# Range check of the decays spread over the later blocks of the second feed-forward, and a prefetch hint on the branch over the general path

## The chip, the cores and the metric

The kernel runs on one core of one Trainium2 chip. The metric is device microseconds for one execution, lower is better. The core has a matrix engine (TensorE, PE in the rows; its weight loads are PEld), a vector engine (VectorE, DVE), a scalar engine (ScalarE, ACT), a general engine (GpSimd, POOL) and a queue engine (SyncE, SP) that issues most transfers. Each engine runs its own instructions in the order in which they stand.

## The reference

A recurrent attention over 768 steps feeds two feed-forward layers. What the change touches is the second feed-forward, and a check on the decays `w` of the recurrence:

```python
def _moe2_ref(x, w_in, w_out):          # x: 3072 x 320, d_ff 2048
    h = np.maximum(x @ w_in, 0.0)
    return (h * h @ w_out).astype(np.float32)
```

The decays are drawn as `rand * 0.1 + 0.85`. The kernel's fast path for the recurrence is meant for decays between 0.25 and 2.0. Outside of that, a slow general path must compute everything again, so the kernel has to look at every one of the 983,040 decays.

## The kernel before, in words

The recurrence, the first feed-forward and the decoding of the weights fill the first 720 us. The weights arrive as 64-bit numbers in tiles `raw`; ACT (L324, L325), DVE (L327, L329) and POOL (L331) turn each into a 32-bit tile `wst`, and ACT and POOL split this into a high and a low part (`wih`, `wil`, `wir` for the first matrix, `wuh`, `wul` for the second).

The second feed-forward runs over 6 token blocks `j` of 512 tokens, and in each over 16 slices `ff` of 128 hidden units. I call one (`j`, `ff`) a step. A step has two halves on PE. `b_h` computes the hidden slice in 8 matmuls into the tile `ph` (L366). ACT and DVE then make its square in two parts: ACT `r_` (L972), DVE `q_` (L973), ACT `rh` (L974), DVE `rl` (L975). `b_o` multiplies `rh` and `rl` with the second matrix in 12 matmuls into four output tiles `po` (L988). `b_o` of a step is written three steps behind its `b_h` (`LAG`). When the last slice of a block is in, the four `po` tiles are copied out to `ob` by DVE and ACT (L998). The last weight tiles are still being decoded while block 0 runs.

`b_load` fetches the tokens of the next block and `b_split` splits them into `xh`, `xl`, `xq` (ACT L353 and L355, DVE L354 and L356).

The check on the decays: `look(i)` loads one eighth of them into `w_` (two buffers) and finds least and largest with two reductions on DVE (L1017). `within()` folds these to one number for each partition (L1023 to L1025), sends it to memory as `ok_d` (L1028), reads it back as one `row` (L1029), and reduces the row to the flag `one` (L1031, L1032). The flag is loaded into a register of each engine (L1043), and `tc.If(fast == 0)` (L1056) branches over the general path.

The program's order within each engine is set by a scheduler, which takes priorities from the order of the code and moves an instruction ahead where its inputs allow. So `look` and `b_split`, written at later places, stand in DVE's order well before the steps beside which they are written.

Of the kernel before, what the change touches and what calls it, by code (L numbers as in the profile page):

```python
# [11 lines left out]
ALU = mybir.AluOpType  # L12
# [13 lines left out]
LEAST, MOST = 0.25, 2.0  # L26
# [33 lines left out]
GAPM = (1300, 900, 1700, 1300, 1600, 1000, 0, 2600)  # L60
GAPE = (1300, 2400, 1700, 1600, 1600, 1300, 1000, 2400)
CUT = (7, 18)
LOOK = (2, 0, 3, 2, 5, 2)
WB = (6, 8, 3)
BP = 6000
BB = (5, 4)
# [176 lines left out]
def body(tc, img, rv, rd, vn, vp, raw, w1, w2, w3t, wo, win, wo2, ident, maskt, out, dbg=None):  # L243
    nc = tc.nc
    mm = nc.tensor.matmul
    act, dve, pool, sp = nc.scalar, nc.vector, nc.gpsimd, nc.sync

    with (
# [12 lines left out]
        with right, tc.manual_schedule(engines={mybir.EngineType.PE}):  # L261
# [90 lines left out]
            def split_x(f2, r2, xh, xl, xq):  # L352
                act.copy(out=xh, in_=f2)  # L353
                dve.tensor_tensor(out=xl, in0=f2, in1=xh, op=ALU.subtract)  # L354
                act.copy(out=xq[:, 0], in_=r2)  # L355
                dve.tensor_tensor(out=xq[:, 1], in0=r2, in1=xq[:, 0], op=ALU.subtract)  # L356

            def dense(ps, w_, ff, xh, xl, xq, i0=0, i1=8):
                h, l, r = w_
                f = slice(128 * ff, 128 * ff + 128)  # L360
                seq = []
                for k in range(2):
                    seq += [(h[:, k, f], xh[:, k]), (h[:, k, f], xl[:, k]), (l[:, k, f], xh[:, k])]
                seq[5:5] = [(r[:, f], xq[:, 0]), (r[:, f], xq[:, 1])]
                for i in range(i0, i1):
                    mm(out=ps, lhsT=seq[i][0], rhs=seq[i][1], start=(i == 0), stop=(i == 7))  # L366
# [123 lines left out]
            with (  # L490
# [30 lines left out]
                q_ = {"prep": sp}  # L521
# [350 lines left out]
                for c in range(NCH):  # L872
                    last = c == NCH - 1
# [52 lines left out]
            def b_split(pl, j, bufs=2):  # L926
                xf, xr = xt[j]
                xh = pl.tile([128, 2, 512], F32R, name="xh2", bufs=bufs)
                xl = pl.tile([128, 2, 512], F32R, name="xl2", bufs=bufs)
                xq = pl.tile([128, 2, 512], F32R, name="xq2", bufs=bufs)  # L930
                split_x(xf, xr, xh, xl, xq)
                xt[j] = (xh, xl, xq)
# [23 lines left out]
        with (  # L956
            left,
            tc.tile_pool(name="mb", bufs=1, side="right") as mb,
            tc.tile_pool(name="ps_h", bufs=4, space=PSUM) as ps_h,
            tc.tile_pool(name="ps_o", bufs=1, space=PSUM) as ps_o,  # L960
        ):
            NB = NTOK // 512
            rr = {}

            def b_h(j, ff):
                ps = ps_h.tile([128, 512], F32, name="ph")
                dense(ps, (wih, wil, wir), ff, *xt[j])
                r_ = mb.tile([128, 512], F32, name="r_", bufs=2)
                q_ = mb.tile([128, 512], F32, name="q_", bufs=2)
                rh = mb.tile([128, 512], F32R, name="rh", bufs=4)  # L970
                rl = mb.tile([128, 512], F32R, name="rl", bufs=4)
                act.activation(out=r_, in_=ps, func=AF.Relu)  # L972
                dve.tensor_tensor(out=q_, in0=r_, in1=r_, op=ALU.mult)  # L973
                act.copy(out=rh, in_=q_)  # L974
                dve.tensor_tensor(out=rl, in0=q_, in1=rh, op=ALU.subtract)  # L975
                rr[ff] = (rh, rl)

            po = {}

            def b_o(j, ff, gs=range(4)):  # L980
                if ff == 0:
                    po[j] = [ps_o.tile([128, DM], F32, name=f"po{g}") for g in range(4)]
                rh, rl = rr[ff]
                for g in gs:
                    t = slice(128 * g, 128 * g + 128)
                    for i, (a_, b_) in enumerate(((rh[:, t], wuh[:, ff]), (rh[:, t], wul[:, ff]),
                                                  (rl[:, t], wuh[:, ff]))):
                        mm(out=po[j][g], lhsT=a_, rhs=b_, start=(ff == 0 and i == 0), stop=(ff == 15 and i == 2))  # L988
                if ff == 15:
                    for g in gs:  # L990
                        c = 4 * j + g
                        if j < NB - 1:
                            ob = mb.tile([128, DM], F32, name="ob", bufs=4)
                        else:
                            if g == 0:
                                po["ob"] = mb.tile([128, 4, DM], F32, name="oball", bufs=1)
                            ob = po["ob"][:, g]
                        (act.copy if g % 2 else dve.tensor_copy)(out=ob, in_=po[j][g])  # L998
                        if j < NB - 1:
                            sp.dma_start(out=out.rearrange("(b s) o -> b s o", b=B)[:, C * c:C * c + C], in_=ob)  # L1000
                    if j == NB - 1 and gs[-1] == 3:
                        for b in range(B):
                            (act if b % 2 else sp).dma_start(
                                out=out.rearrange("(b c s) o -> b s c o", b=B, s=C)[b][:, 4 * j:4 * j + 4],
                                in_=po["ob"][C * b:C * b + C])

            NW = 8
            nw = NU * S * D // 128 // NW
            low, high = (mb.tile([128, NW], F32, name=n, bufs=1) for n in ("low", "high"))

            def look(i):

                w_ = mb.tile([128, nw], F32, name="w_", bufs=2)
                sp.dma_start(out=w_, in_=raw[3].rearrange("u s d -> (u s d)").rearrange("(p f) -> p f", p=128)[
                    :, nw * i:nw * i + nw])
                for o, op in ((low, ALU.min), (high, ALU.max)):
                    dve.tensor_reduce(out=o[:, i:i + 1], in_=w_, axis=mybir.AxisListType.X, op=op)  # L1017

            def within():


                for o, op in ((low, ALU.min), (high, ALU.max)):
                    dve.tensor_reduce(out=o[:, 0:1], in_=o, axis=mybir.AxisListType.X, op=op)  # L1023
                dve.tensor_scalar(out=high[:, 0:1], in0=high[:, 0:1], scalar1=MOST, scalar2=None, op0=ALU.is_le)
                dve.scalar_tensor_tensor(out=low[:, 0:1], in0=low[:, 0:1], scalar=LEAST, in1=high[:, 0:1],  # L1025
                                         op0=ALU.is_ge, op1=ALU.mult)
                row = mb.tile([1, 128], F32, name="row", bufs=1)
                sp.dma_start(out=ok_d, in_=low[:, 0:1])  # L1028
                sp.dma_start(out=row, in_=ok_d.rearrange("p o -> o p"))  # L1029
                one = mb.tile([1, 1], mybir.dt.int32, name="one", bufs=1)  # L1030
                dve.tensor_reduce(out=row[:, 0:1], in_=row, axis=mybir.AxisListType.X, op=ALU.min)  # L1031
                dve.tensor_copy(out=one, in_=row[:, 0:1])  # L1032
                return one

            lag = []
            for j in range(NB):
                for ff in range(16):
                    if j == LOOK[0] and LOOK[1] <= ff < NW + LOOK[1]:
                        look(ff - LOOK[1])
                    if (j, ff) == LOOK[2:4]:  # L1040
                        fast = within()
                    if (j, ff) == LOOK[4:6]:
                        fast = nc.values_load(fast, min_val=0, max_val=1)  # L1043
                    if ff == 4 and j + 1 < NB:
                        b_load(mb, j + 1)
                    if ff == 12 and j + 1 < NB:
                        b_split(mb, j + 1)
                    b_h(j, ff)
                    lag.append((j, ff))
                    if len(lag) > LAG:  # L1050
                        b_o(*lag.pop(0))
            for g in range(4):
                with tc.high_priority(offset=FIRST * (4 - g)):
                    for it in lag:
                        b_o(*it, gs=(g,))
        with tc.If(fast == 0):  # L1056
            general(tc, raw, w1, w2, w3t, wo, win, wo2, ident, out)
        if dbg is not None:
            sp.dma_start(out=dbg["X"], in_=X_d)
# [57 lines left out]
```

## Time and profile before

| what | value |
|---|---|
| median of 3 runs | 1101.18 us (1099.33 to 1102.74) |
| profiled execution, its own time | 1096.26 us |
| its span, first to last instruction | 1094.4 us |
| PE busy | 922.8 us (84%) |
| DVE busy | 735.0 us (67%) |
| ACT busy | 454.1 us (41%) |
| POOL busy | 264.6 us (24%) |

All rows come from the one profiled execution. A busy share says how long an engine had work under way, not whether that work set the end. "idle before <-" in a row is the time that the engine stood still before it, and what ended the wait.

### The profile page before, as it was taken

What the parts mean: (1) busy time and instruction counts of PE and PEld (TensorE: products, weight loads), DVE (VectorE), ACT (ScalarE), POOL (GpSimd) and SP (SyncE); (2) the same over time, 40 slices, a digit from 0 to 9 for tenths busy, and PEclk for the clock granted to TensorE, in tenths of its full rate; (3) what the DMA queues carried; (4) which work ended last, traced back from release to release, by engine and by line L of the source; (5) the groups of instructions that cost most, each with busy time, mean ns of one, the idle gap of its engine ahead of it and who ended that gap; (6) DMA issues with size and microseconds to landing.
All of it is one profiled execution on the core that took longest, in us unless ns stands there. A gap on an engine that the chain in (4) does not pass through costs nothing.

```text
span 1094.4 us, 29719 instructions
## 1 busy us (share of the span) xinstructions
PE 922.8 (84%) x12240; PEld 826.5 (76%) x12240; DVE 735.0 (67%) x1467; ACT 454.1 (41%) x1022; POOL 264.6 (24%) x310
## 2 busy tenths in 40 slices
PE   1326766789979889987999989888989999999996
PEld 1224544588879878887898879777878989898985
DVE  7785989967975996788489434999834434343432
ACT  3423655443434433433343434766423334343331
POOL 0384777613121122312100000886200000000000
PEclk9999988889989989989999989999989999999999
DMA  8967767377656656756555442569300200000001
GB/s 225 272 193 220 206 200 194 93 203 195 150 146 162 173 142 184 190 136 161 140 132 116 118 107 58 152 170 203 90 25 5 50 1 25 1 25 1 23 2 27
DMA packets 214743, 134.48 MB, mean 123 GB/s; under 512 B 143415, under 2 KB 187576, under 8 KB 214184
## 3 DMA queue, kind: packets, MB, share of 16 engines
q1 hardware_dynamic: 214312, 132.18, 46.5%
q8 instruction: 98, 1.61, 0.6%
q10 hardware_dynamic: 288, 0.33, 0.1%
q14 instruction: 45, 0.37, 0.1%
HBM read 99.27 MB, written 33.19 MB: 121 GB/s over the span
## 4 chain that ended last, share of the span: by engine, by line
PE 36%; DVE 9%; DMA 3%; issue 3%; ACT 1%; POOL 1%; SPq 0%; DVEq 0%; ACTq 0%; POOLq 0%
PE po L988 14%; PE ph L366 13%; PE ab L366 4%; PE px L424 2%; PE pat L795 1%; DVE wst L329 1%; DVE wst L327 1%; PE pat L767 1%; DVE high L1017 1%; DVE rl L975 1%; DMA X_d<-yst 1%; DVE tmp L651 1%; DMA ok_d<-low 1%; DVE gl L404 1%; DVE T L654 1%
## 5 line engine op out<-in xcount | busy, mean ns | idle before, releaser
L988 PE MATMUL po<-wuh,rh 128*128 128x320 f32 x384 | 119.0, 312 | 4.7 <-DVE ob L998 3.3
L988 PE MATMUL po<-wuh,rl 128*128 128x320 f32 x384 | 114.3, 311 | 6.1 <-DVE rl L975 6.1
L988 PE MATMUL po<-wul,rh 128*128 128x320 f32 x384 | 118.9, 311 | 0.0
L403 ACT CAST gh<-g 128x256 fp32r<-128x256 f32 x96 | 38.9, 406 | 108.0 <-DVE g L398 107.7
L331 POOL TENSOR_TENSOR wst<-wst,raw 128x256 f32<-128x256 f32 (+1 forms) x72 | 70.2, 982 | 55.0 <-DVE wst L329 32.0
L988 PEld LDWEIGHTS po<-wuh,rh 128*128 128x128 f32 x384 | 72.9, 190 | 9.1 <-issue 3.8
L366 PE MATMUL ab<-xh,w1h 128*128 128x256 f32 x192 | 60.9, 317 | 22.2 <-DVE g L398 22.2
L988 PEld LDWEIGHTS po<-wuh,rl 128*128 128x128 f32 x384 | 71.8, 190 | 7.9 <-DVE rl L975 7.3
L366 PE MATMUL ph<-xh,wih 128*128 128x512 f32 x192 | 76.0, 396 | 1.6 <-POOL wst L331 1.6
L988 PEld LDWEIGHTS po<-wul,rh 128*128 128x128 f32 x384 | 73.0, 190 | 4.0
L366 PE MATMUL ph<-xh,wil 128*128 128x512 f32 x192 | 76.0, 396 | 0.0
L366 PE MATMUL ph<-xl,wih 128*128 128x512 f32 x192 | 75.7, 394 | 0.0
L651 DVE TENSOR_TENSOR tmp<-PT,T 128x31 f32<-128x31 f32 (+20 forms) x170 | 69.1, 407 | 3.4
L795 PE MATMUL pat<-YI,YR 128*40 128x72 f32 (+1 forms) x1536 | 56.8, 236 | 15.4 <-DVE qt L597 10.4
L654 DVE TENSOR_TENSOR T<-T,tmp 128x31 f32<-128x31 f32 (+20 forms) x170 | 67.5, 397 | 2.7
L795 PEld LDWEIGHTS pat<-YI,YR 128*40 128x40 f32 x1536 | 52.4, 124 | 20.3 <-DVE qt L597 11.7
L404 DVE TENSOR_TENSOR gl<-g,gh 128x256 fp32r<-128x256 f32 x96 | 46.4, 484 | 27.7 <-ACT gh L403 27.3
L424 PE MATMUL px<-wph,gh 128*128 128x320 f32 x192 | 64.8, 338 | 0.0
L424 PE MATMUL px<-wph,gl 128*128 128x320 f32 x192 | 61.0, 318 | 1.3 <-DVE gl L404 1.3
L397 ACT COPY a_sb<-ab 128x256 f32<-128x256 f32 x96 | 35.6, 371 | 63.0 <-PE ab L366 62.4
L424 PE MATMUL px<-wpl,gh 128*128 128x320 f32 x192 | 60.7, 316 | 0.0
L366 PE MATMUL ph<-xq,wir 128*128 128x512 f32 x192 | 60.3, 394 | 0.0
(535 smaller groups left out, 2519.3 us busy)
## 6 DMA issues: line engine op xcount, KB each, us to landing
im<-img SPq DMA_DIRECT2D x38, 240.0 KB
raw<-w3t SPq DMA_DIRECT2D x32, 256.0 KB
KB_d<-kn SPq DMA_DIRECT2D x24, 320.0 KB
YR<-KB_d SPq DMA_DIRECT2D x48, 160.0 KB
AW_d<-wi SPq DMA_DIRECT2D x24, 214.5 KB
wt<-AW_d SPq DMA_DIRECT2D x24, 214.5 KB
raw<-wo SPq DMA_DIRECT2D x16, 320.0 KB
RX<-vp SPq DMA_DIRECT2D x24, 208.0 KB
```

The source lines that it names most:

```text
L327: dve.tensor_scalar(out=ou, in0=ou, scalar1=3, scalar2=0x7FFFFFFF, op0=ALU.logical_shift_left, op1=ALU.bitwise_and)
L329: dve.scalar_tensor_tensor(out=ou, in0=lo, scalar=29, in1=ou, op0=ALU.logical_shift_right, op1=ALU.bitwise_or)
L331: pool.tensor_tensor(out=o, in0=o, in1=hi.bitcast(F32), op=ALU.mult)
L366: mm(out=ps, lhsT=seq[i][0], rhs=seq[i][1], start=(i == 0), stop=(i == 7))
L397: act.copy(out=a_sb, in_=ps[:, 0])
L403: act.copy(out=t["gh"][:, ff], in_=g)
L404: dve.tensor_tensor(out=t["gl"][:, ff], in0=g, in1=t["gh"][:, ff], op=ALU.subtract)
L424: mm(out=ps, lhsT=a_, rhs=b_, start=(k == 0 and i == 0), stop=(k == 7 and i == 2))
L651: dve.tensor_tensor(out=tv, in0=Pv[:, :, s, s + 1:n].unsqueeze(3).to_broadcast(sh), in1=Tv[:, :, s, 0:s + 1].unsqueeze(2).to_broadcast(sh) ...
L654: return dve.tensor_tensor(out=o, in0=o, in1=tv, op=ALU.subtract).ins
L795: mm(out=ps[64 * y:64 * y + D, b, 72 * z:72 * z + n], lhsT=YR[:, u], rhs=YI[:, u, 0:n], start=True, stop=True, tile_position=(0, 64 * y))
L988: mm(out=po[j][g], lhsT=a_, rhs=b_, start=(ff == 0 and i == 0), stop=(ff == 15 and i == 2))
```

## The change

The reductions of `look` and `within` become a generator with one piece at a time: from step (1, 1) on, after each second step, one piece is taken. A piece is one reduction, and `tc.issue_after(last[1])` puts it behind the `rl` of the step just written on DVE. Between the write of `ok_d` and the reduction of `row` four empty pieces are taken, that is eight steps. `b_split` is put behind the `rh` (on ACT) and the `rl` (on DVE) of the step before. And the branch over the general path gets a label and a hint "LikelyTaken" on SP, ACT and DVE. Nothing is computed that was not computed before, and the pieces' instructions are the same.

```diff
-LOOK = (2, 0, 3, 2, 5, 2)
+LOOK = (1, 0, 2, 1, 5, 2)
...
-            rr = {}
+            tc.mark_branch_hint_location("wide", hint="LikelyTaken",
+                                         engines=[mybir.EngineType.SP, mybir.EngineType.Activation,
+                                                  mybir.EngineType.DVE])
+            rr, last = {}, []
...
-                act.copy(out=rh, in_=q_)
-                dve.tensor_tensor(out=rl, in0=q_, in1=rh, op=ALU.subtract)
+                last[:] = [act.copy(out=rh, in_=q_).ins,
+                           dve.tensor_tensor(out=rl, in0=q_, in1=rh, op=ALU.subtract).ins]
...
                 for o, op in ((low, ALU.min), (high, ALU.max)):
-                    dve.tensor_reduce(out=o[:, i:i + 1], in_=w_, axis=mybir.AxisListType.X, op=op)
+                    with tc.issue_after(last[1]):
+                        dve.tensor_reduce(out=o[:, i:i + 1], in_=w_, axis=mybir.AxisListType.X, op=op)
+                    yield
...
                 sp.dma_start(out=row, in_=ok_d.rearrange("p o -> o p"))
+                for _ in range(4):
+                    yield
                 one = mb.tile([1, 1], mybir.dt.int32, name="one", bufs=1)
-                dve.tensor_reduce(out=row[:, 0:1], in_=row, axis=mybir.AxisListType.X, op=ALU.min)
-                dve.tensor_copy(out=one, in_=row[:, 0:1])
-                return one
+                with tc.issue_after(last[1]):
+                    dve.tensor_reduce(out=row[:, 0:1], in_=row, axis=mybir.AxisListType.X, op=ALU.min)
+                    dve.tensor_copy(out=one, in_=row[:, 0:1])
+                yield one
+
+            def guard():
+                for i in range(NW):
+                    yield from look(i)
+                yield from within()
...
                     if ff == 12 and j + 1 < NB:
-                        b_split(mb, j + 1)
+                        with tc.issue_after(last[0]), tc.issue_after(last[1]):
+                            b_split(mb, j + 1)
                     b_h(j, ff)
+                    if LOOK[0:2] <= (j, ff) and ff % LOOK[2] == LOOK[3]:
+                        fast = next(steps, fast)
...
-        with tc.If(fast == 0):
+        with tc.If(fast == 0, label="wide"):
```

What moves, engine by engine, at three places. In the new program line numbers are a few higher (L976 and L978 are `q_` and `rl`, L1021 the reductions), and the numbers in names differ.

First, DVE in block 0, before. From the split of the tokens of block 2 (`xl_11769`) to the `rl` of step (0, 6), whose square is `q__11103`; `q__11074` is that of step (0, 5).

```order
L354 TENSOR_TENSOR xl_11769<-xf_11522,xh_11768 128x1024
L975 TENSOR_TENSOR rl<-q__11074,rh 128x512
L327 TENSOR_SCALAR wst<-wst 128x320
L973 TENSOR_TENSOR q__11103<-r__11102 128x512
L1017 TENSOR_REDUCE low<-w__11891 128x1
L329 SCALAR_TENSOR_TENSOR wst<-raw,wst 128x320
L1017 TENSOR_REDUCE high<-w__11891 128x1
L356 TENSOR_TENSOR xq_11770<-xr_11523,xq_11770 128x512
L327 TENSOR_SCALAR wst<-wst 128x320
L1017 TENSOR_REDUCE low<-w__11924 128x1
L1017 TENSOR_REDUCE high<-w__11924 128x1
L975 TENSOR_TENSOR rl<-q__11103,rh 128x512
```

The same place in the new program, from the `rl` of step (0, 5) (`q__11077`) to that of step (0, 6) (`q__11106`):

```order
L978 TENSOR_TENSOR rl<-q__11077,rh 128x512
L976 TENSOR_TENSOR q__11106<-r__11105 128x512
L327 TENSOR_SCALAR wst<-wst 128x320
L329 SCALAR_TENSOR_TENSOR wst<-raw,wst 128x320
L327 TENSOR_SCALAR wst<-wst 128x256
L978 TENSOR_TENSOR rl<-q__11106,rh 128x512
```

Only decoding is left between them; the splits and all reductions are gone from block 0, but for the split of block 1, which now stands behind the `rl` of step (0, 11).

Second, DVE at the end of the check, before. `q__11429` is the square of the first steps of block 1, `po_11005` an output tile of block 0.

```order
L1025 SCALAR_TENSOR_TENSOR low<-low,high 128x1
L975 TENSOR_TENSOR rl<-q__11371,rh 128x512
L975 TENSOR_TENSOR rl<-q__11400,rh 128x512
L973 TENSOR_TENSOR q__11429<-r__11428 128x512
L1031 TENSOR_REDUCE row<-row 1x1
L975 TENSOR_TENSOR rl<-q__11429,rh 128x512
L1032 CAST one<-row 1x1
L998 COPY ob<-po_11005 128x320
```

The new program has the reduction of `row` in block 3, 8 pairs of `q_` and `rl` behind the row that makes `low` for `ok_d`:

```order
L976 TENSOR_TENSOR q__12735<-r__12734 128x512
L978 TENSOR_TENSOR rl<-q__12735,rh 128x512
L1040 TENSOR_REDUCE row<-row 1x1
L1041 CAST one<-row 1x1
L976 TENSOR_TENSOR q__12767<-r__12766 128x512
L978 TENSOR_TENSOR rl<-q__12767,rh 128x512
```

Before, an `rl` and the copies `ob` stood right behind it and one `q_` ahead of it after `low`; now eight whole steps lie between.

Third, where the reductions stand now on DVE, in block 1 (`w__11439` is the first eighth of the decays):

```order
L978 TENSOR_TENSOR rl<-q__11505,rh 128x512
L1021 TENSOR_REDUCE high<-w__11439 128x1
L976 TENSOR_TENSOR q__11553<-r__11552 128x512
L978 TENSOR_TENSOR rl<-q__11553,rh 128x512
L976 TENSOR_TENSOR q__11582<-r__11581 128x512
L978 TENSOR_TENSOR rl<-q__11582,rh 128x512
L1021 TENSOR_REDUCE low<-w__11589 128x1
```

There is one reduction after each second `rl`. The hints stand as the second instruction of SP, ACT and DVE, at the very start of the program; the branch is row 817 of SP, 959 of ACT and 1396 of DVE.

## Rows read from the trace of the kernel before

**Rows 1.** Windows: busy us of each engine by stretch, granted clock, DMA share.

```profile
731.00:741.00 10.00, 7.75 (x45) 6.75 (x44) 9.90 (x13) 8.13 (x18) 7.15 (x7) 1.00 1.02 206
751.00:761.00 10.00, 7.27 (x39) 6.26 (x40) 10.00 (x15) 5.89 (x15) 4.60 (x5) 1.00 0.98 203
...
791.00:801.00 10.00, 6.65 (x33) 5.50 (x33) 2.18 (x6) 1.40 (x4) 0.00 (x0) 0.91 0.00 0
801.00:811.00 10.00, 10.00 (x48) 9.39 (x48) 4.50 (x8) 4.29 (x8) 0.00 (x0) 0.75 0.22 68
```

**Rows 2.** The chain that ended last, its last matmuls: start, length, what.

```profile
1075.37 1.87 PE ph L366 x8
1077.24 7.05 PE po L988 x48
```

**Rows 3.** Timeline of PE, its rows with idle time: start, length, what, [idle].

```profile
721.37 0.47 PE L366 MATMUL ph<-xh,wih 128*128 128x512 f32 x1 [1.64 <-POOL wst L331]
...
735.34 0.71 PE L988 MATMUL po<-wuh,rl 128*128 128x320 f32 x3 [2.00 <-DVE rl L975]
738.87 0.42 PE L988 MATMUL po<-wuh,rl 128*128 128x320 f32 x1 [0.25 <-DVE rl L975]
752.30 0.41 PE L988 MATMUL po<-wuh,rl 128*128 128x320 f32 x1 [2.39 <-DVE rl L975]
760.30 0.85 PE L988 MATMUL po<-wuh,rl 128*128 128x320 f32 x4 [1.44 <-DVE rl L975]
770.67 0.42 PE L988 MATMUL po<-wuh,rh 128*128 128x320 f32 x1 [1.40 <-ACT rh L974]
...
800.30 0.61 PE L988 MATMUL po<-wuh,rh 128*128 128x320 f32 x1 [3.35 <-DVE ob L998]
```

**Rows 4.** Instructions of line L1056, the branch: count, ns, first and last start.

```profile
L1056 SPq EVENT_SEMAPHORE  x8: 17/17/17, 1090.7 to 1091.2; - x8
...
L1056 SPq COMPARE_BRANCH  x1: 50/50/50, 1085.6 to 1085.6; - x1
...
L1056 ACTq COMPARE_BRANCH  x1: 54/54/54, 1087.6 to 1087.6; - x1
...
L1056 ACTq EVENT_SEMAPHORE  x1: 17/17/17, 1090.9 to 1090.9; - x1
```

**Rows 5.** Timeline of DVE in block 0.

```profile
738.74 1.75 DVE L354 TENSOR_TENSOR xl<-xf,xh 128x1024 fp32r<-128x1024 f32 x1
...
743.07 1.23 DVE L356 TENSOR_TENSOR xq<-xr,xq 128x512 fp32r<-128x512 f32 x1
...
749.88 1.21 DVE L354 TENSOR_TENSOR xl<-xf,xh 128x1024 fp32r<-128x1024 f32 x1
751.01 1.23 DVE L975 TENSOR_TENSOR rl<-q__11074,rh 128x512 fp32r<-128x512 f32 x1
...
754.08 1.14 DVE L1017 TENSOR_REDUCE low<-w__11891 128x1 f32<-128x960 f32 x1
...
759.56 0.68 DVE L975 TENSOR_TENSOR rl<-q__11103,rh 128x512 fp32r<-128x512 f32 x1
```

**Rows 6.** Timeline of DVE in a late step.

```profile
1064.83 0.69 DVE L975 TENSOR_TENSOR rl<-q__13795,rh 128x512 fp32r<-128x512 f32 x1 [0.69 <-ACT rh L974]
...
1067.07 0.69 DVE L973 TENSOR_TENSOR q__13824<-r__13823 128x512 f32<-128x512 f32 x1 [1.55 <-ACT r__13823 L972]
```

**Rows 7.** Timeline of DVE around the reduction of `row`.

```profile
788.45 0.15 DVE L1025 SCALAR_TENSOR_TENSOR low<-low,high 128x1 f32<-128x1 f32 x1
...
798.82 0.27 DVE L1031 TENSOR_REDUCE row<-row 1x1 f32<-1x128 f32 x1 [8.31 <-DMA row<-ok_d]
799.02 0.67 DVE L975 TENSOR_TENSOR rl<-q__11429,rh 128x512 fp32r<-128x512 f32 x1
```

**Rows 8.** Line L1113, the end of the program, on SP: stretches 1090:1092 and 1092:1095.

```profile
L1113 SPq EVENT_SEMAPHORE  x2: 28/28/28, 1091.3 to 1091.4; - x2
...
L1113 SPq EVENT_SEMAPHORE  x8: 17/28/28, 1092.9 to 1094.4; - x8
```

More of the change, by code (lines that the diff above doesn't have):

```diff
@@ L1016, in look @@
                 for o, op in ((low, ALU.min), (high, ALU.max)):
-                    dve.tensor_reduce(out=o[:, i:i + 1], in_=w_, axis=mybir.AxisListType.X, op=op)
+                    with tc.issue_after(last[1]):
+                        dve.tensor_reduce(out=o[:, i:i + 1], in_=w_, axis=mybir.AxisListType.X, op=op)
+                    yield
             def within():
[L1022 to L1026, printed above, removed]
+                with tc.issue_after(last[1]):
+                    for o, op in ((low, ALU.min), (high, ALU.max)):
+                        dve.tensor_reduce(out=o[:, 0:1], in_=o, axis=mybir.AxisListType.X, op=op)
+                    dve.tensor_scalar(out=high[:, 0:1], in0=high[:, 0:1], scalar1=MOST, scalar2=None, op0=ALU.is_le)
+                    dve.scalar_tensor_tensor(out=low[:, 0:1], in0=low[:, 0:1], scalar=LEAST, in1=high[:, 0:1],
+                                             op0=ALU.is_ge, op1=ALU.mult)
                 row = mb.tile([1, 128], F32, name="row", bufs=1)
@@ L1029, in within @@
                 sp.dma_start(out=row, in_=ok_d.rearrange("p o -> o p"))
+                for _ in range(4):
+                    yield
                 one = mb.tile([1, 1], mybir.dt.int32, name="one", bufs=1)
-                dve.tensor_reduce(out=row[:, 0:1], in_=row, axis=mybir.AxisListType.X, op=ALU.min)
-                dve.tensor_copy(out=one, in_=row[:, 0:1])
-                return one
-            lag = []
+                with tc.issue_after(last[1]):
+                    dve.tensor_reduce(out=row[:, 0:1], in_=row, axis=mybir.AxisListType.X, op=ALU.min)
[5 more added lines that the diff above has]
+                yield from within()
+            lag, steps, fast = [], guard(), None
             for j in range(NB):
                 for ff in range(16):
[L1038 to L1041, printed above, removed]
                     if (j, ff) == LOOK[4:6]:
```

## Prediction

> **What bounds the kernel now.** The change lies in the second feed-forward and behind it, so I read that stage alone. First the windows, ten microseconds each, to see which engine is full where. In block 0 (731 to 761 us) DVE is busy for 9.9 and 10.0 of 10 us and PE for only 7.75 and 7.27; the transfer engines are full there as well (share 1.02 and 0.98). In 791 to 801 us both stand still for much of the time: PE 6.65, DVE 2.18 [rows 1].
>
> Second the chain at the end, for the pace that PE can hold. Eight `ph` matmuls take 1.87 us, and 48 `po` matmuls 7.05 us, so 12 take 1.76 [rows 2]. A step is 3.63 us, and the 96 steps of the stage are 348.5 us. PE starts the first at 721.37 [rows 3] and is done with the last at 1077.24 + 7.05 = 1084.29 [rows 2]: 362.9 us. So PE loses 14.4 us in the stage, and what the change can bring on PE is a part of that.
>
> Third the timeline of PE, for where they are lost. After the first matmul six rows have idle time [rows 3]: 2.00 + 0.25 (735 and 739 us), 2.39 + 1.44 + 1.40 (752, 760 and 771 us), and 3.35 (800 us), together 10.8 us. The idle is counted from the end of a matmul of 0.31 us, but the next one normally starts 1.76 / 12 = 0.15 us after its start, so each gap costs 0.16 us more: 1.0 for six. [...] Everything else in the stage is dense.
>
> Last the end of the program: PE is done at 1084.3 and the span ends at 1094.4. SP branches at 1085.6 and its next instruction, one of eight waits, starts at 1090.7. ACT branches at 1087.6 and goes on at 1090.9, though that instruction has no transfer to wait for [rows 4].
>
> **The change, part by part.**
>
> Block 0. The waits at 752, 760 and 771 us are for `rl` (twice) and `rh`, the results of DVE's queue. Ahead of the `rl` that ends at 752.2 stand three instructions that leave the place: `xl` 1.75, `xq` 1.23 and `xl` 1.21 [rows 5], 4.2 us, against a wait of 2.39. Ahead of the `rl` that starts at 759.56 stand, besides these, four reductions of 1.14 [rows 5] and another `xq`, 5 us or more, against 1.44. Between there and 771 us the order of before has four further reductions, 4.6 us, against 1.40; the `rh` there waits for a `q_` of DVE. So each of the three waits is smaller than the work that leaves from in front of it, and I take all of it: 5.23 + 3 x 0.16 = 5.7 us. At least it is nothing, if DVE only waits elsewhere (a rival below), and at most 5.7. The waits at 735 and 739 us come before the first moved instruction; 2.25 us stay, and nothing is taken for them.
>
> What the reductions cost where they go. 16 of them at 1.14 us are 18.2 us of DVE. A late step has one gap of 1.55 us on DVE, between the end of `rl` and the next `q_` [rows 6], and one reduction stands just there, in each second step. It fits: DVE needs 4 x 0.69 + 1.14 = 3.9 us in two steps of 7.26. Twice a reduction stands ahead of the copies `ob`, whose tile PE needs after nine more `po` and eight `ph` matmuls, 9 x 0.15 + 1.87 = 3.2 us; that covers 1.14. `b_split` behind an `rl` is 1.2 + 0.7 = 1.9 us, in one place with a reduction 3.0, so the next `q_` is up to 1.5 us late; `rl` is needed three steps later, and that hides it. Without this cover it would be 16 x 1.14 at the very most. I take 0.
>
> The loads of the decays: six of the eight move out of block 0 into steps where almost nothing is moved. On SP they stand behind the tokens of a later block and the writes of the block just done, with two buffers, so a load is issued some six steps (20 us) ahead of its reduction. 0 on the path.
>
> The wait for `row`. Now DVE ends `low` at 788.6 us and the row is back at 798.82; DVE stood 8.31 us at the reduction of `row`, with `rl` and both `ob` copies behind it in its queue, and PE stood 3.35 us for the `ob` [rows 3, 7]. In the new order eight steps, 29 us, lie between; the round trip took 10.2 [rows 7]. On SP the read of `row` stands behind one write of `ob`, a step at most. So this wait goes: 3.35 + 0.16 = 3.5 us. And the clock, which fell behind this idle time, stays up if PE does not stand still there: 2.5 us. If it fell anyway, it would be 0.
>
> The hint. SP's first wait behind the branch is for the last output transfers, which no hint makes faster: it starts at 1090.7 and there I take nothing. But SP has a second stop: two instructions of the end at 1091.3 and 1091.4, the third only at 1092.9 [rows 8], with nothing to wait for that was not long there. [...] ACT's 3.3 us stop ends ahead of SP's last, so it is worth nothing. [...]
>
> [...]
>
> The sum: 5.7 + 3.5 + 2.5 + 1.4 = 13.1 us. The profiled execution took 1096.26, so one like it would take 1083.2. The median of the runs is 4.9 us above it; nothing moves ahead of 720 us, so I take the same difference off the median: 1101.18 - 13.1 = **1088.1 us**.
>
> **The rivals.**
>
> The hint does nothing. For it: it stands 815 instructions ahead of the branch on SP and more on the others. [...] Gain 11.7, time 1089.5. [...]
>
> DVE stays late in block 0. It takes its instructions in order, and ahead of an `rl` there still stands the decoding of a weight tile; if that tile is late (the transfer engines' share is 0.98 to 1.02 there [rows 1]), the `rl` waits with it. For it: the waits at 735 and 739 us [rows 3] have no moved instruction before them, and an `rl` takes 1.23 us there when POOL works beside it, against 0.68 without [rows 5]. Against: in the new order ten token transfers fewer stand ahead of the last weight tiles on SP. Then the 5.7 us are lost: gain 7.4, time 1093.8.
>
> It gets slower. A reduction reaches its turn before its load is there, DVE stands as it did for `row`, and what stands behind (`q_`, `rl`, `ob`) comes late to PE. Eight loads; PE has about two steps of cover, 7 us. To eat 13.1 us and 3.3 more each load must cost PE 2 us, that is land 9 us after its turn: 1088.1 + 8 x 2 = 1104.1. Against it: the 20 us lead, and transfer engines that move next to nothing after 801 us but for the token loads.
>
> **How the numbers follow.** Forecast 0.57; hint without effect 0.18; DVE late in block 0 0.17; slower 0.04; something that leaves it unchanged, as a new wait at a block's end with the clock fallen again, 0.04. About 0.3% (3.3 us) is what a measurement of this kernel can tell from no change. The first three are faster by more than that, 0.92; same 0.04; slower 0.04. The range reaches up to 1094 (1093.8 of the second rival) and down to 1083: 1088.1 less the 2.6 us of the two early waits, less 0.9 at the end, less the 1.85 by which the fastest run lies under the median gives 1082.8.
>
> **What would show it.** PE's rows without idle time at 752, 760, 771 and 800 us (shifted), and with some 2 us at 735; a granted clock of 1.00 from the first step to the last; DVE well under 10 of 10 us in 751 to 771; 18 us of reductions spread over blocks 1 and 2 with no wait in front; the last matmul some 11.7 us earlier than 1084.3; and behind the branch ACT going on at once, SP's eight instructions of the end in one piece, and 8.7 us instead of 10.1 from the last matmul to the end. Wrong it would be if PE waits for `rl` elsewhere in block 0, or if DVE waits for a load of decays.

## The result, and the profile after

The changed kernel takes 1092.19 us (median of 15 runs, 1084.16 to 1100.96) where the kernel before, beside it on the same chip, takes 1102.47 (15 runs, 1095.75 to 1107.85). The medians lie 10.3 us apart; the comparison of the undisturbed runs gives a ratio of 0.9911, with a 95% interval of 0.9893 to 0.9930: 9.8 us less, between 7.7 and 11.8. The forecast was 1088.1 us, 13.1 us less. So the time fell into the range and on the forecast side, but the sum was too large by more than the interval.

The profiled execution after has a span of 1097.2 us, longer than the 1094.4 of the profile before. That difference lies ahead of the changed stage: TensorE starts the second feed-forward at 733.32 us here and at 721.37 before [rows 3], although nothing of the change but the hint stands ahead of there. In the 14 profiles of this study the start lies between 720.65 and 733.32 us, and for two executions of this one kernel at 733.32 and 727.98. So I compare the stage and the end, not spans.

The timeline of PE after, its rows with idle time in the stage (start, length, what, [idle]), answers to [rows 3]:

```profile
733.32 0.47 PE L366 MATMUL ph<-xh,wih 128*128 128x512 f32 x1 [1.66 <-POOL wst L331]
748.09 0.71 PE L991 MATMUL po<-wuh,rl 128*128 128x320 f32 x3 [2.60 <-DVE rl L978]
771.51 0.42 PE L991 MATMUL po<-wuh,rh 128*128 128x320 f32 x1 [0.91 <-ACT rh L977]
773.18 0.57 PE L991 MATMUL po<-wuh,rl 128*128 128x320 f32 x1 [1.11 <-DVE rl L978]
```

The end of the chain that ended last, as [rows 2]:

```profile
1082.95 7.05 PE po L991 x48
```

The last matmul ends at 1082.95 + 7.05 = 1090.00, so the stage takes 356.7 us instead of 362.9, and against the 348.5 us of 96 dense steps it loses 8.2 instead of 14.4. The wait of 3.35 us for `ob` has no successor: behind 773 us PE has no idle row. In block 0 three waits stay, 4.62 us, and with them the clock fell. Windows after (busy us of PE, PEld, DVE, ACT, POOL, then granted clock, DMA share, GB/s), as [rows 1]:

```profile
743.00:753.00 10.00, 7.40 (x34) 6.14 (x33) 9.90 (x14) 7.54 (x19) 7.90 (x9) 0.83 1.07 238
763.00:773.00 10.00, 8.16 (x44) 6.81 (x43) 9.90 (x13) 6.24 (x16) 8.58 (x9) 1.00 0.36 103
773.00:783.00 10.00, 9.82 (x47) 9.08 (x48) 6.83 (x11) 5.42 (x12) 5.52 (x5) 0.83 0.00 1
```

Twice the granted clock is 0.83 over 10 us; in slices of 1 to 2 us it is 0.50 in 750 to 752 and in 774 to 776 us, and 1.00 in 743 to 749 and 777 to 781. If PE loses pace in proportion, which is my estimate, that is 2 x 0.17 x 10 = 3.4 us. With 4.62 + 3 x 0.16 of waits that makes 8.5, against 8.2 from the stage's length. And DVE is as full as before, 9.90 of 10 us, until the decoding is done. What stands ahead of the late `rl` now, in the timeline of DVE from the `rl` of step (0, 6) to that of step (0, 7):

```profile
766.03 0.69 DVE L978 TENSOR_TENSOR rl<-q__11106,rh 128x512 fp32r<-128x512 f32 x1
766.63 1.11 DVE L329 SCALAR_TENSOR_TENSOR wst<-raw,wst 128x256 uint32<-128x256 uint32 x1
767.67 0.97 DVE L327 TENSOR_SCALAR wst<-wst 128x256 uint32<-128x256 uint32 x1
768.67 0.86 DVE L329 SCALAR_TENSOR_TENSOR wst<-raw,wst 128x256 uint32<-128x256 uint32 x1
769.45 1.35 DVE L976 TENSOR_TENSOR q__11135<-r__11134 128x512 f32<-128x512 f32 x1
770.72 0.85 DVE L327 TENSOR_SCALAR wst<-wst 128x320 uint32<-128x320 uint32 x1
771.61 0.91 DVE L329 SCALAR_TENSOR_TENSOR wst<-raw,wst 128x320 uint32<-128x320 uint32 x1
772.45 0.68 DVE L978 TENSOR_TENSOR rl<-q__11135,rh 128x512 fp32r<-128x512 f32 x1
```

No idle time in brackets: DVE waited for no tile, it was decoding them, ahead of `q_` and ahead of `rl` of the same step. Five instructions of decoding take 4.7 us here, with POOL busy for 6.03 of the 6.42 us. The reduction of `row` stands behind an `rl` and found its data there (no idle; before, 8.31 us [rows 7]):

```profile
947.15 0.69 DVE L978 TENSOR_TENSOR rl<-q__12735,rh 128x512 fp32r<-128x512 f32 x1 [0.69 <-ACT rh L977]
947.76 0.27 DVE L1040 TENSOR_REDUCE row<-row 1x1 f32<-1x128 f32 x1
```

The instructions of the branch (L1070) and of the program's end (L1127) after, with count, ns, first and last start, as [rows 4, 8]:

```profile
L1070 SPq EVENT_SEMAPHORE  x8: 17/17/17, 1095.2 to 1095.9; - x8
L1070 DVEq COMPARE_BRANCH  x1: 90/90/90, 1090.6 to 1090.6; - x1
L1070 DVEq EVENT_SEMAPHORE  x1: 21/21/21, 1091.2 to 1091.2; - x1
L1070 SPq COMPARE_BRANCH  x1: 70/70/70, 1091.4 to 1091.4; - x1
L1070 ACTq COMPARE_BRANCH  x1: 68/68/68, 1093.0 to 1093.0; - x1
L1070 ACTq EVENT_SEMAPHORE  x1: 17/17/17, 1093.4 to 1093.4; - x1
...
L1127 SPq EVENT_SEMAPHORE  x10: 17/28/28, 1095.9 to 1097.2; - x10
```

ACT goes on 0.4 us after its branch instead of 3.3, DVE 0.6 us, and SP's ten instructions of the end come in one piece. From SP's first wait behind the branch to the end of the span it is 1097.2 - 1095.2 = 2.0 us; before it was 1094.4 - 1090.7 = 3.7 [rows 4, 8].

### The profile page after: what moved, and what is told of

The parts are those of the page before. It is cut to its first block, busy times and chain, and to the rows that moved or that the text cites. A ratio compares the mean times of both kernels' runs of the same rounds, so it can differ in the third digit from the quotient of the medians.

```text
span 1097.2 us, 29717 instructions
## 1 busy us (share of the span) xinstructions
PE 926.6 (84%) x12240; PEld 831.3 (76%) x12240; DVE 741.6 (68%) x1467; ACT 454.9 (41%) x1022; POOL 260.5 (24%) x310
## 4 chain that ended last, share of the span: by engine, by line
PE 41%; DVE 10%; DMA 3%; issue 2%; ACT 1%; SPq 0%; POOL 0%; ACTq 0%; DVEq 0%; POOLq 0%
PE ph L366 14%; PE po L991 14%; PE ab L366 5%; PE px L424 2%; DVE wst L327 1%; PE pat L795 1%; DVE T L654 1%; DVE tmp L651 1%; DVE wst L329 1%; PE pat L767 1%; DMA xf<-X_d 1%; PE pat L780 1%; DVE gl L404 1%; DVE RX L803 1%; DMA X_d<-yst 1%
## 5 line engine op out<-in xcount | busy, mean ns | idle before, releaser
L991 PE MATMUL po<-wuh,rl 128*128 128x320 f32 x384 | 117.9, 310 | 3.7 <-DVE rl L978 3.7
L795 PE MATMUL pat<-YI,YR 128*40 128x72 f32 (+1 forms) x1536 | 59.4, 242 | 14.0 <-DVE qt L597 12.7
L795 PEld LDWEIGHTS pat<-YI,YR 128*40 128x40 f32 x1536 | 54.9, 128 | 18.7 <-DVE qt L597 14.2
L366 PEld LDWEIGHTS ab<-xh,w1h 128*128 128x128 f32 x192 | 38.6, 201 | 32.8 <-DVE g L398 31.1
```

The costliest lines, as they stand in the source:

```text
L795: mm(out=ps[64 * y:64 * y + D, b, 72 * z:72 * z + n], lhsT=YR[:, u], rhs=YI[:, u, 0:n], start=True, stop=True, tile_position=(0, 64 * y))
```

## The experiments

Two theories stood when the first runs were chosen. **Queue**: in block 0 DVE has a backlog of decoding, so what leaves its queue there only lets decoding run ahead; all that the stage gained is the wait for `row` with the clock behind it. **Masked**: leaving block 0 gave its 5.7 us, and the clock, lower in that one execution, ate it. One table holds the measurements. Stage is from the first `ph` to the end of the last `po`, from PE's timeline and the chain as above; lost is the stage less 348.5; end is the rest of the span. The ratio is to the kernel before on the same chip.

| kernel | stage us | lost | end us | ratio, 95% interval |
|---|---|---|---|---|
| before | 362.9 | 14.4 | 10.1 | |
| changed | 356.7 | 8.2 | 7.2 | 0.9911 (0.9893 to 0.9930) |
| after_again | 354.7 | 6.2 | 8.3 | 0.9923 (0.9894 to 0.9953) |
| row_late | 362.8 | 14.3 | 9.4 | 0.9997 (0.9974 to 1.0021) |
| hint_only | 362.1 | 13.6 | 7.4 | 1.0002 (0.9984 to 1.0021) |
| row_at_once | 354.6 | 6.1 | 8.2 | 0.9912 (0.9881 to 0.9943) |
| one_look | 356.7 | 8.2 | 8.2 | 0.9915 (0.9885 to 0.9945) |
| paced | 352.1 | 3.6 | 8.2 | 0.9887 (0.9855 to 0.9918) |
| q_first | 354.5 | 6.0 | 8.2 | 0.9923 (0.9900 to 0.9946) |
| no_hint | 354.6 | 6.1 | 8.8 | 0.9952 (0.9925 to 0.9979) |
| row_behind | 356.8 | 8.3 | 10.3 | 0.9939 (0.9920 to 0.9959) |
| no_split | 359.5 | 11.0 | 8.4 | 0.9963 (0.9940 to 0.9985) |
| paced5 | 349.7 | 1.1 | 7.3 | 0.9857 (0.9832 to 0.9883) |
| paced4 | 350.4 | 1.9 | 8.2 | 0.9847 (0.9819 to 0.9874) |

**row_late**, the kernel before with one edit:

```
                 sp.dma_start(out=row, in_=ok_d.rearrange("p o -> o p"))
+                return row
+
+            def decide(row):
+
                 one = mb.tile([1, 1], mybir.dt.int32, name="one", bufs=1)
                 dve.tensor_reduce(out=row[:, 0:1], in_=row, axis=mybir.AxisListType.X, op=ALU.min)
...
                         fast = within()
+                    if (j, ff) == (LOOK[2], LOOK[3] + 4):
+                        fast = decide(fast)
```

> The kernel before, with the reduction of the row moved four steps behind its transfer and nothing else; reductions stay in block 0, no hint. Theory 'queue' (freeing VectorE in block 0 only lets the weight decoding run ahead, so all of the gain of the second feed-forward, 6.2 us between the two profiles, is the wait for the row and the slow clock behind it): stage from first ph to last po matmul 357 us instead of 362.9, loss up to 790 us unchanged at 8 us, ratio to before 0.994 to 0.995. Rival 'masked' (leaving block 0 gave its 5.7 us, and lower clock in that one execution ate it): the same 6 us here, so this run alone does not tell the two apart, but with 'masked' the whole change should give 12 us plus the stop in other executions. Rival 'price of the wait' (only the 3.5 us of idle time is bought, the clock comes back by itself): 359.4 us, ratio 0.997.

Nothing moved: lost 14.3, ratio 0.9997. The text places the reduction of `row` four steps later, but the scheduler put it where it had been, ahead of the same `rl`, and DVE's timeline shows the same wait:

```profile
804.72 0.27 DVE L1035 TENSOR_REDUCE row<-row 1x1 f32<-1x128 f32 x1 [8.48 <-DMA row<-ok_d]
804.92 0.67 DVE L975 TENSOR_TENSOR rl<-q__11429,rh 128x512 fp32r<-128x512 f32 x1
```

So this run tests no theory; it shows that the new place in the text did not move this instruction.

**row_behind** does what row_late was meant to do, with a rule of order (`last[0]` is the `rl` of the step just written):

```
-                dve.tensor_reduce(out=row[:, 0:1], in_=row, axis=mybir.AxisListType.X, op=ALU.min)
-                dve.tensor_copy(out=one, in_=row[:, 0:1])
+                with tc.issue_after(last[0]):
+                    dve.tensor_reduce(out=row[:, 0:1], in_=row, axis=mybir.AxisListType.X, op=ALU.min)
+                    dve.tensor_copy(out=one, in_=row[:, 0:1])
...
                     b_h(j, ff)
+                    if (j, ff) == LOOK[2:4]:
+                        fast = decide(fast)
```

> The kernel before with its 16 reductions where they stood, and only the reduction of the row and its conversion tied behind an rl of block 3 (row_late changed the place in the text but the scheduler left the reduction where it was). If row wait and slow clock behind it are worth what the loss accounting says: loss beyond 60 us of the feed-forward 0 instead of 5.3 to 6.1, loss in its first 60 us unchanged at 8 to 9, feed-forward 356.5 to 357.5 us, ratio to before 0.994 to 0.9955. Rival (leaving block 0 buys most of it): feed-forward 361 us or more, ratio 0.998 or above.

As the accounting says. The waits of block 0 are those of before, and none follows (PE's timeline, rows with idle time):

```profile
737.75 0.71 PE L988 MATMUL po<-wuh,rl 128*128 128x320 f32 x3 [2.00 <-DVE rl L975]
748.36 0.41 PE L988 MATMUL po<-wuh,rl 128*128 128x320 f32 x1 [0.15 <-DVE rl L975]
754.72 0.42 PE L988 MATMUL po<-wuh,rl 128*128 128x320 f32 x1 [2.48 <-DVE rl L975]
762.71 0.85 PE L988 MATMUL po<-wuh,rl 128*128 128x320 f32 x4 [1.43 <-DVE rl L975]
773.09 0.42 PE L988 MATMUL po<-wuh,rh 128*128 128x320 f32 x1 [1.40 <-ACT rh L974]
```

7.46 + 5 x 0.16 = 8.3 us lost, where before lost 14.4: the row's wait and the clock behind it are 6.1 us of the stage, and 6.7 us of the timed runs (0.9939 of 1098.86, interval 4.5 to 8.8). It is the largest single part of the change.

**row_at_once**, the changed kernel without the four empty pieces (eight steps) of distance:

```
-                for _ in range(4):
-                    yield
```

> The changed kernel with the four steps between the row's transfer and its reduction taken out; reductions spread over blocks 1 and 2 and the hint stay. 'Queue': the wait for the row comes back in block 3, the feed-forward takes 361 to 363 us, end 7.3 us, ratio to before 0.996 to 0.998 (the hint alone). 'Masked': block 0 gives 5.7 us where the clock does not fall there, feed-forward 357 us, ratio 0.992.

Neither theory's account of it: the ratio, 0.9912, is the one that masked gave, but the stage takes 354.6 us and not 357, and DVE stands 7.1 us at the row. DVE's timeline:

```profile
914.65 0.48 DVE L1001 COPY ob<-po 128x320 f32<-128x320 f32 x1
915.42 0.69 DVE L978 TENSOR_TENSOR rl<-q__12505,rh 128x512 fp32r<-128x512 f32 x1 [0.29 <-ACT rh L977]
923.22 0.27 DVE L1038 TENSOR_REDUCE row<-row 1x1 f32<-1x128 f32 x1 [7.10 <-DMA row<-ok_d]
```

PE has no idle row anywhere near it. The wait of 7.1 us costs nothing here, and one of 8.31 cost 3.5 and the clock before [rows 3, 7], because of what stood behind it: there an `rl` and two `ob` copies of the block just done, here the next step's `q_`, with both `ob` copies and the `rl` ahead. PE needs a step's `rl` three steps after its `ph`, and three steps are 10.9 us. So the place in the queue is enough to take the cost away; the distance is not needed for it.

**after_again**, the changed kernel a second time.

> The changed kernel a second time, for a second profile. 'Queue': loss in block 0 (idle time and slow clock, first 55 us of the feed-forward) again 7 to 9 us, feed-forward 356 to 358 us. 'Masked': where the clock does not fall in block 0, its loss is 2 to 5 us and the feed-forward 350 to 353 us.

Between the two: lost 6.2 us, with the clock at 1.00 throughout. PE's timeline:

```profile
741.95 0.71 PE L991 MATMUL po<-wuh,rl 128*128 128x320 f32 x3 [2.00 <-DVE rl L978]
745.48 0.41 PE L991 MATMUL po<-wuh,rl 128*128 128x320 f32 x1 [0.26 <-DVE rl L978]
757.25 0.41 PE L991 MATMUL po<-wuh,rl 128*128 128x320 f32 x1 [0.64 <-DVE rl L978]
765.40 0.41 PE L991 MATMUL po<-wuh,rh 128*128 128x320 f32 x1 [1.01 <-ACT rh L977]
767.07 0.42 PE L991 MATMUL po<-wuh,rl 128*128 128x320 f32 x1 [1.12 <-DVE rl L978]
```

This pair, row_behind and after_again, both with the clock up, measures block 0: 8.3 us lost with the splits and reductions there, 6.2 without (6.1 in row_at_once and no_hint). The gain is 2.1 us, not 5.7 and not 0 (the waits alone, 7.46 and 5.03 us, would give 2.4). The 2.00 and 0.25 at the front stay, as forecast. Before, PE waited 2.39 us for step (0, 5), 1.44 for (0, 6) and 1.40 for (0, 9); now it waits 0.64 for (0, 5), and 1.01 + 1.12 for (0, 7), where it did not wait before.

**no_split**, the changed kernel without the rule that keeps the next block's split behind `rl`:

```
-                        with tc.issue_after(last[0]), tc.issue_after(last[1]):
-                            b_split(mb, j + 1)
+                        b_split(mb, j + 1)
```

> The changed kernel without the rule that puts the split of the next block's input behind rl; the scheduler then pulls xl and xq of blocks 1 and 2 (1.2 and 0.7 us each, and the two ScalarE copies of each) in among the decoded tiles of block 0. 'Queue' (what stands ahead of rl in VectorE's order of block 0 is paid for in part): loss in the first 60 us 8 to 10 us instead of 6.1, feed-forward 356.5 to 358.5 us, ratio 0.993 to 0.995. If the split's place is free, as the prediction costed it: 354.6 us, ratio 0.991 to 0.992.

Lost 11.0, ratio 0.9963. The scheduler pulls `xl` and `xq` of blocks 1 and 2 in among the decoded tiles. DVE's timeline, and the row of PE that waits longest:

```profile
749.28 1.21 DVE L354 TENSOR_TENSOR xl<-xf,xh 128x1024 fp32r<-128x1024 f32 x1
750.42 1.22 DVE L978 TENSOR_TENSOR rl<-q__11077,rh 128x512 fp32r<-128x512 f32 x1
```

```profile
758.49 0.64 PE L991 MATMUL po<-wuh,rl 128*128 128x320 f32 x1 [2.95 <-DVE rl L978]
```

Its four waits are 1.99, 0.16, 2.50 and 2.95 us, 8.2 with 0.16 each, as much as in row_behind, although no reduction stands in block 0; the rest is clock (0.84 granted in 751 to 761 us, 0.82 in 761 to 771). So with the splits still there, taking the reductions out bought next to nothing, and taking the splits out as well bought the 2.1 us. A kernel with the reductions in block 0 and the splits out was not run, so what the splits alone are worth is not shown.

**one_look** leaves 14 reductions out:

```
                     with tc.issue_after(last[1]):
-                        dve.tensor_reduce(out=o[:, i:i + 1], in_=w_, ...)
+                        if i == 0:
+                            dve.tensor_reduce(out=o, in_=w_.rearrange(...), ...)
```

> The changed kernel with 14 of the 16 reductions of 128x640 values left out (only the first piece of the decays is looked at, the loads stay). 'Queue' and the prediction (reductions cost nothing at their new place): feed-forward as the changed kernel, 356 to 357 us, ratio to before 0.991. Rival 'price' (each spread reduction delays q or rl of a step by part of its 0.7 to 1.4 us): feed-forward 345 to 354 us, ratio 0.98 to 0.989.

0.9915 against 0.9911: at their new place the reductions (of 128x960 values each; the expectation has 128x640) cost nothing that can be measured. Its 8.2 us lost are block 0 with one fall of the clock, to 0.83 in 765 to 775 us; without that fall's 1.7 us (0.17 x 10, the same estimate) they are 6.5, where after_again lost 6.2 with all reductions.

**hint_only** and **no_hint** put the hint alone on the kernel before, and take it alone from the changed one:

```
+            tc.mark_branch_hint_location("wide", hint="LikelyTaken", engines=[...])
...
-        with tc.If(fast == 0):
+        with tc.If(fast == 0, label="wide"):
```

> The kernel before with the hint and the label of the branch, nothing else. If the hint buys what the two profiles differ by: last matmul to end 7.3 us instead of 10.15, feed-forward unchanged at 363 us, ratio 0.997. If only SP's second stop goes, as predicted: 8.7 us, ratio 0.9987. If the hint does nothing: stops of 3 to 4 us stay on VectorE and ScalarE, 10.1 us, ratio 1.000.

> The changed kernel without the hint and the label. Last matmul to end 10.1 us instead of 7.3 with stops of 3 to 4 us on VectorE, ScalarE and SP behind the branch, feed-forward 356.7 us, ratio to before 0.9937 (0.9911 and 2.9 us of 1102). If the landings of the output and not the hint gave the difference: 7.3 us and 0.991.

The end is 10.1, 9.4, 8.8 and 10.3 us in the four profiles without the hint, and 7.2 to 8.4 in the ten with it. It scatters with the landing of the last output: from SP's last issue to its first wait 5.6 us in before, 4.3 in no_hint, and 4.3 and 5.4 in the two executions of the changed kernel. What lies behind that first wait does not scatter. In row_behind, without the hint, from line L1063's first wait and line L1120, the program's end:

```profile
L1063 SPq EVENT_SEMAPHORE  x8: 17/17/17, 1087.1 to 1087.6; - x8
...
L1120 SPq EVENT_SEMAPHORE  x10: 17/28/28, 1087.7 to 1090.8; - x10
```

1090.9 - 1087.1 = 3.8 us, 3.7 in before and row_late, 1086.4 - 1082.8 = 3.6 in no_hint; with the hint 2.0 in each of the ten profiles, as 1091.0 - 1089.0 in after_again. By the profiles the hint is worth 1.7 us. The timed ratio of hint_only, 1.0002 with 0.2% to each side, cannot tell 0.15% from nothing, but it excludes the 0.997 of its first expectation; no_hint against after_again, 0.9952 to 0.9923, points the right way but their intervals overlap. Behind its branch DVE stands 0.6 to 0.7 us in all ten, against 4.2 to 4.4 without the hint. ACT does not follow so: its stop is 0.4 to 0.5 us in six of the ten, but 2.5 in hint_only, 3.6 in one_look, 3.0 in q_first and 3.1 in no_split, against 2.5 to 3.9 without.

**paced**, **q_first**, **paced5** and **paced4** ask whether block 0's waits come from the order of DVE's queue ("queue") or from the sum of its work ("sum of work"). paced and its kin keep the staging pool of the weights open and write the decoding of the last groups into block 0, one tile behind each step's `rl` (here paced5; paced has groups 6 and 7 from step 3 on, paced4 groups 4 to 7 from step 0; `hold` is what puts a tile's two DVE instructions behind that `rl`):

```
-            for j in range(8):
+            def late():
+                hold[:] = [None]
+                for j in range(5, 8):
+                    for k in range(2):
+                        hold[:] = last[1:]
+                        split_w(wst, win, wih, wil, j, k)
+                        yield
+                for j in range(5, 8):
+                    for k in (2 * j, 2 * j + 1):
+                        hold[:] = last[1:]
+                        wu(wst, k)
+                        yield
+
+            for j in range(5):
...
                     b_h(j, ff)
+                    if j == 0 and ff >= 1:
+                        for _ in range(1):
+                            next(tiles, None)
```

> The changed kernel with the decoding of the last two of eight weight groups (8 tiles) written into block 0, one tile behind the rl of each step from (0,3) on. 'Queue' (VectorE's order, not its sum of work, makes the waits in block 0): the idle time of TensorE behind q, rh and rl of steps (0,6) and (0,7) goes (2 us and the slow clock behind it), feed-forward 352 to 355 us against 356.7, ratio to before 0.985 to 0.989. [...]

> The changed kernel with relu, q, rh and rl of block 0 at a higher priority for the scheduler, so that rl stands one decoded tile earlier in VectorE's order at some steps. 'Queue': part of the 5 us of idle time in block 0 goes, feed-forward 353 to 356 us, ratio to before 0.988 to 0.990. 'Sum of work': no change, 356.7 us, ratio 0.991.

> As paced, with the last three weight groups (12 tiles) paced, from step (0,1) on. 'Queue': the two small waits that paced kept at 39 and 51 us go, the first wait (2.1 and 0.4 us at 14.0 and 17.5 us) stays since its order is the same; loss 2.5 to 3.5 us, feed-forward 351 to 352 us, ratio 0.986 to 0.988. 'Sum of work': tiles come late, loss 4 us or more.

> As paced, with the last four weight groups (16 tiles) paced, from step (0,0) on, so that rl of step (0,1) stands behind half a decoded tile less. 'Queue': the first wait shrinks below 1 us as well, loss 0.5 to 2 us, feed-forward 349 to 350.5 us, ratio 0.984 to 0.987. 'Sum of work': the tiles of the last groups come late and TensorE waits for them at steps 8 to 15, loss 4 us or more, feed-forward 352.5 us or more.

q_first, relu to `rl` under `tc.high_priority(offset=FIRST)` in block 0, changed the order in a few places and the time not at all (lost 6.0): inconclusive, since `rl` was still behind whole tiles. The paced ones are clear: 3.6, 1.1 and 1.9 us lost. paced5 lost less than the 2.5 to 3.5 us of its expectation, which had thought the first wait unchanged; it is the only one left in the stage, and half as long (PE's timeline):

```profile
737.54 0.56 PE L1003 MATMUL po<-wuh,rl 128*128 128x320 f32 x2 [1.08 <-DVE rl L990]
```

paced4 lost that one too and got three, of 0.48, 0.48 and 0.30 us, for the tiles of its last groups (`wuh` and `wul`): there tiles begin to come late. Windows 20 to 40 us into the stage, of row_at_once and of paced5:

```profile
749.00:759.00 10.00, 9.36 (x53) 8.20 (x52) 9.93 (x13) 7.12 (x16) 8.53 (x9) 1.00 0.95 205
759.00:769.00 10.00, 7.94 (x44) 6.62 (x43) 9.86 (x14) 6.70 (x16) 8.58 (x9) 1.00 0.19 65
```

```profile
745.00:755.00 10.00, 10.00 (x57) 8.98 (x56) 7.88 (x12) 8.28 (x18) 6.90 (x8) 1.00 0.84 200
755.00:765.00 10.00, 10.00 (x58) 9.11 (x57) 6.80 (x12) 6.74 (x14) 5.26 (x6) 1.00 0.21 72
```

Over the stage both decode the same 16 tiles on DVE, but in these 20 us row_at_once decodes nine and paced5 six; paced5 starts the last one 53 us into the stage, row_at_once 40 us into it. So DVE has room between them and PE is full. Order and spacing, then, make the waits. But the work is not the same either: the 16 tiles take DVE 24.6 us in row_at_once, 20.3 in paced5 and 15.9 in paced4 (L327 and L329, the first 70 us), and POOL, beside which a decoding instruction of 0.31 us mostly took 0.77 to 1.01 before and after (L327, 128x320), is busy for 34.3 of the 40 us from 729 us on in row_at_once, for 34.9 of the 50 from 725 us on in paced5, and for 34.4 of the 70 from 727 us on in paced4. No run separates the two. paced5 (0.9857) and paced4 (0.9847) are also the fastest kernels here, 6 and 7 us below the changed one by their ratios; their intervals do not tell them apart.

## Why the prediction was right, and where not

**Right in direction and in three of the four terms, too large in the fourth.** Forecast terms and what the runs showed: block 0 5.7 us, measured 2.1 (row_behind against after_again); the row's wait 3.5 and the clock behind it 2.5, together 6.0, measured 6.1 (before against row_behind); the hint 1.4, measured 1.7; reductions at their new place 0, measured 0 (one_look). 2.1 + 6.1 + 1.7 = 9.9, and the timed runs say 9.8, between 7.7 and 11.8. No run shows the 2.5 or the 1.4 as the forecast had them: in their place stand the 6.1 us of wait and clock together, and the 1.7 us behind SP's first wait.

**The step that failed** is in block 0: "each of the three waits is smaller than the work that leaves from in front of it, and I take all of it". That holds only if the rest of DVE's queue keeps its order and its pace, and it kept neither. DVE had a backlog: its windows show 9.9 of 10 us before and after. When the splits and reductions left, decoding moved up a little: from the stage's start on, 22, 25 and 30 instructions of decoding stand ahead of the `rl` of steps (0, 5), (0, 6) and (0, 7), where 20, 23 and 29 stood. And it became slower, which the forecast had not counted at all. Before, the same stretch from the `rl` of step (0, 6) to that of (0, 7) was (DVE's timeline; the `rl` ahead of it starts at 759.56 [rows 5]):

```profile
760.76 0.49 DVE L327 TENSOR_SCALAR wst<-wst 128x256 uint32<-128x256 uint32 x2
761.17 0.48 DVE L329 SCALAR_TENSOR_TENSOR wst<-raw,wst 128x320 uint32<-128x320 uint32 x1
761.57 0.32 DVE L327 TENSOR_SCALAR wst<-wst 128x320 uint32<-128x320 uint32 x1
...
762.41 0.75 DVE L329 SCALAR_TENSOR_TENSOR wst<-raw,wst 128x256 uint32<-128x256 uint32 x2
763.08 0.68 DVE L975 TENSOR_TENSOR rl<-q__11132,rh 128x512 fp32r<-128x512 f32 x1
```

Six instructions of decoding took 2.0 us there, with POOL busy for 1.35 of 3.52 us; after, five take 4.7, with POOL busy for 6.03 of 6.42. Over the first 70 us of the stage the same 16 tiles take DVE 19.0 us before and 24.6 in after_again. A reduction lasts 1.14 us beside POOL and without it; a decoding instruction of one form (L327, 128x320) 0.31 us where POOL stood idle, and mostly 0.77 to 1.01 beside it. So of the 14.0 us of splits and reductions that left from ahead of the three waits (the `xl`, `xq` and eight reductions of 1.14 us in DVE's timeline to 770 us), 5.6 came back as slower decoding, and 2.8 us of waiting stand where 5.2 stood, most of it at step (0, 7). That PE waits for `rl` elsewhere in block 0 is a sign of being wrong that the forecast itself had named. No run separates how much of the 2.8 us is what moved up and how much the slower pace. The forecast had set the splits against the first of the three waits and the reductions above all against the other two; with the reductions gone and the splits left in (no_split) the waits sum to 8.2 us, as before.

**The rival that came closest** was "DVE stays late in block 0", with the right symptom and the wrong cause. Its time, 1093.8 us, is also nearer to the measured 1092.2 than the forecast's 1088.1. It spoke of tiles that are late because the transfer engines are full (share 0.95 to 1.07 in 743 to 763 us of the profile after). DVE had no idle time there, so no tile was late; and paced5 has no wait in 745 to 765 us, with the transfer engines at 0.84 in the first half of it.

**The row.** The term was right, for a reason of which the forecast had only half. It counted eight steps of distance; row_at_once has none of the added eight, waits 7.1 us and loses nothing. Before, the price came from the two `ob` copies and the `rl` behind the wait.

**The clock.** "1.00 from the first step to the last" was wrong for the profiled execution (two windows at 0.83 in block 0) and right for after_again and row_at_once, whose granted clock is 1.00 through the stage. The forecast's 2.5 us is an estimate, the granted clock of 0.75 in 801 to 811 us [rows 1] taken as pace lost; with the waits it makes 10.8 + 1.0 + 2.5 = 14.3 of the 14.4 us lost before. At the new place of the row the clock did not fall: it is 1.00 from 783 to 1090 us in the profile after, where PE is busy for 306.99 of 307 us.

**The hint.** The forecast took 1.4 us for SP's second stop and left its first wait as it was. No run shows what the stop consists of; the profiles show that it went, and 3.7 us from SP's first wait to the end became 2.0. Its range also took off 0.9 us at the end, which no run shows; the landings of the output scatter by more than a microsecond with the hint and without. The rival in which the hint does nothing has the ten profiles against it: SP's second stop [rows 8] is gone in all of them, and DVE's stop behind the branch falls from 4.2 or more to 0.7 us or less. The forecast's other sign, ACT going on at once, held in six of the ten only. How the hint works is not shown.

## What to carry to other kernels

Taking work from in front of a wait in an engine's queue bought less than the wait while that engine was full (DVE busy 9.9 of 10 us): 2.1 us for 14 us of work. Ask what moves up and what becomes slower beside another engine (L327, 128x320: 0.31 us without POOL, mostly 0.77 to 1.01 beside it), and tie the filler work behind the urgent result instead (paced5: 1.1 us lost of 6.1). What the wait for the row cost was decided by what stood behind it: 8.31 us ahead of two copies and an `rl` cost 6.1 us, 7.10 us behind them cost nothing. And where a scheduler sets the order, a line moved in the text may move nothing (row_late); look at the order before counting a gain.

## What the runs showed that I had not expected

The granted clock in block 0 differs between executions with the same waits: behind a wait of 2.00 us it stayed at 1.00 in before and after_again, and behind one of 2.01 us it fell in hint_only. The window there:

```profile
739.00:749.00 10.00, 9.58 (x45) 8.58 (x46) 9.90 (x13) 5.95 (x15) 6.43 (x6) 0.83 0.90 190
```

By the estimate above (0.17 x 10) each such fall to 0.83 over 10 us costs 1.7 us, so a single profile can hide or invent a gain of that size; what decides it stays open. Also open is why the stages ahead, which nothing of the change touches, end 5.3 us apart in two executions of the changed kernel (733.32 and 727.98).
